# One load for the filter of two blocks, the last block's h turned by transfers, and a new table of places, in a long-convolution and SwiGLU kernel

## The chip, the cores and the metric

The kernel runs on one core of one Trainium2 chip. The core has five engines that run side by side, each through its own queue of instructions in order: TensorE (PE; its weight loads are PEld) multiplies matrices, VectorE (DVE) and ScalarE (ACT) work on elements, GpSimd (POOL) does small things here and issues transfers, SyncE (SP) only issues transfers. An instruction that waits holds up all that stand behind it on its engine, and nothing on the others. Transfers run on 16 DMA engines that all queues share. The metric is the device time of one execution in microseconds (us); lower is better.

## What is computed

The input `A_q` is 2048 rows of 640 channels, in bfloat16. A gated long convolution and a residual give `h`, and a SwiGLU feed-forward on the normalised `h` gives the output:

```
def _A_ref(q, k, v, shift_k, ssm_k, ssm_D):
    ...
        k_shift = k_shift + k_pad[:, t:t + S, :] * shift_k[:, ks - 1 - t][None, None, :]
    kv = k_shift * v
    ...
    y = irfft(rfft(kv padded to 2S) * rfft(ssm_k padded to 2S))[:S]
    y = y + kv * ssm_D[None, None, :]
    return q * y
def _B_ref(x, w_gate, w_up, w_down):
    g = _silu(x @ w_gate)
    u = x @ w_up
    return (g * u) @ w_down
h = x + _A_ref(_layernorm(x), A_k, A_v, A_shift_k, A_ssm_k, A_ssm_D)
h2 = h + _B_ref(_layernorm(h), B_w_gate, B_w_up, B_w_down)
```

(The transforms are written shorter here than in the source.) D is 640, the hidden width F is 1728.

## The kernel before

The 2048 rows are cut into 4 blocks of 512 (`NB`, `BLK`). For each block j the kernel computes a spectrum `G{j}` of the filter `A_ssm_k` and a spectrum `X{j}` of `kv`, both as products with a cosine and sine basis on TensorE (`forward`, line 324) that ScalarE or VectorE copies out of the accumulators (`taken`, line 310: the casts and activations of line 319). `window` joins the spectra of two neighbouring filter blocks to `H{j}`. `mac` (line 524) multiplies: block j needs the sum over i of `X{i}` times `H{j-i}`, so block 0 has one pair and block 3 has four. `inverse` (line 651) goes back to rows with products on TensorE (line 698), then takes the gate, the residual and the statistics of the second normalisation. `turn_h` (line 717) normalises the four row groups of h and lays channels on partitions (`hT`), and `ffn` (line 751) does gate and up (line 769), silu and product (lines 783 to 787), and down (lines 833 and 845). The feed-forward of block j-1 is written beside the convolution of block j, so that TensorE has work while the other engines prepare the next block.

Nothing of this order is left to a compiler. Each step is an entry of `Plan`, and the table `ORDER` (line 47) lists the entries in the order in which they are emitted; every engine runs its own in that order. A negative entry takes the step's other form, on another engine: a copy out of the accumulators goes from ScalarE to VectorE, a load goes from SyncE's to GpSimd's queue, and an addition on VectorE becomes a transfer from GpSimd's queue that adds into its destination:

```
    def added(ns, fn, to, what, reads, write, n=1):
        plan.add("dve", ns, fn, reads, [write], ("add", 2 * P * R * D * n, lambda: nc.gpsimd.dma_start(out=to(), in_=what(), accum_op=ALU.add, ...)))
```

Such an adding transfer (line 243 in the profile) moves 128 x 2560 bfloat16 elements, 655,360 bytes, within SBUF. `mac` is the main user of `added`, through `plus` (line 544; line 545 where it stays on VectorE). For block 3 it makes two strings of additions that each wait for the one ahead: six into the half-size buffer `acc`, and six into the accumulator `A`, three into each of its parts:

```
                    if not i:
                        plus(total, parts[1][0], acc, parts[1][1])
                ...
                for get, at in parts[:1] if final else parts:
                    plus(total, get, acc, at)
                    ...
                        plus(lambda sin=sin: A.part(sin), lambda b=b: flat2(b), A.at(sin), b)
            dve(1402, lambda: v.tensor_sub(A.part(0), A.part(0), A.part(1)), [A.at(1)], [A.at(0)])
            dve(1402, lambda: v.tensor_add(A.part(1), total(), parts[1][0]()), [acc, parts[1][1]], [A.at(1)])
```

The terms that are added are products of `one` (line 542). After the last two lines (581 and 582), `inverse` takes a difference and a sum (662 and 663), two more of half the size (674) and two of the same size (677) before its products can read.

The filter of block j comes by `load_g` (line 289), channels on partitions, 512 columns of 2 bytes, so rows of 1 KB. `g_turned` (line 415) lays time on partitions. For block 0 TensorE turns it (`transposed`, line 411, with a copy out at line 413); for blocks in `GTURN` ScalarE first reorders the whole block (line 419) and SyncE issues four transposing transfers (`turns`, line 404). `HTURN` says the same for h: blocks 1 and 2 are turned by transfers, blocks 0 and 3 by TensorE. Buffers come from an arena of 22 units, and accumulators (`ps`) from four tiles.

Of the kernel before, what the change touches and what calls it, by code (L numbers as in the profile page):

```python
# [16 lines left out]
D = 640  # L17
FF = 1728
P = 128
BLK = 512  # L20
NB = S_TOT // BLK
R = BLK // P
L = 2 * BLK
EPS = 1e-5
KT = D // P
# [14 lines left out]
HTURN = (1, 2)  # L40
# [151 lines left out]
def kernel(ctx: ExitStack, tc: tile.TileContext, A_q, A_k, A_v, A_shift_k, A_ssm_k, A_ssm_D, B_x,  # L192
# [9 lines left out]
             "scr": ("p (a d) -> p a d", {"a": 4}), "hT": ("p (k t) -> p k t", {"k": KT}),  # L202
# [11 lines left out]
    def new(kind):  # L214
        return Buf("U", kind, None, 2 if kind == "S" else 1) if kind in views else Buf(kind, kind)
# [71 lines left out]
    def load_g(j):  # L287
        b = new("ld")
        load(MB, lambda q: q.dma_start(
            out=ap(b).rearrange("p (c t) -> p c t", c=KT),  # L290
            in_=A_ssm_k[0:D, j * BLK:(j + 1) * BLK].rearrange("(c p) t -> p c t", p=P)), [b])
        return b
# [113 lines left out]
    def transposed(pieces, reads, to, write):  # L406
# [5 lines left out]
        pe(290, tr, reads + [ident], [pt])  # L412
        evict(lambda copy: copy(to(), turned(pt)[:, 0:D].rearrange("p (c t) -> p c t", c=KT)), [pt], [write], other=407)

    def g_turned(g, j):
        gT = new("t4")
        if j in GTURN:
            by_r = new("scr")
# [572 lines left out]
```

## Time and profile before

| what | value |
|---|---|
| device time, median of 3 runs (lowest, highest) | 251.36 us (251.21, 253.07) |
| profiled execution, span from first to last instruction | 251.4 us |
| granted TensorE clock, mean | 1.000 |
| busy: PE, DVE, ACT, POOL | 237.3, 197.7, 173.9, 54.0 us |
| instructions: PE, DVE, ACT, POOL | 2113, 249, 300, 54 |
| DMA: GpSimd's queue, SyncE's queue | 11.96 MB, 21.38 MB |
| their packets' time, as a share of 16 engines' span | 25.9%, 32.1% |

The profile is one execution taken by the hardware profiler, so its times add up to its own span of 251.4 us, which here is the median of the runs within 0.1 us. Busy times overlap. A busy TensorE is not one at its peak, since matmuls are pipelined and a slow one counts as busy. A view of waits gives what ended the idle time ahead of an instruction; the chain of waits goes back from the last instruction, at each step to what released it. The view of stretches gives the busy time of each engine in a piece of the span, with the count of its instructions in brackets.

### The profile page before, as it was taken

What the parts mean: (1) busy time and instruction counts of PE and PEld (TensorE: products, weight loads), DVE (VectorE), ACT (ScalarE), POOL (GpSimd) and SP (SyncE); (2) the same over time, 40 slices, a digit from 0 to 9 for tenths busy, and PEclk for the clock granted to TensorE, in tenths of its full rate; (3) what the DMA queues carried; (4) which work ended last, traced back from release to release, by engine and by line L of the source; (5) the groups of instructions that cost most, each with busy time, mean ns of one, the idle gap of its engine ahead of it and who ended that gap; (6) DMA issues with size and microseconds to landing.
All of it is one profiled execution on the core that took longest, in us unless ns stands there. A gap on an engine that the chain in (4) does not pass through costs nothing.

```text
span 251.4 us, 5138 instructions
## 1 busy us (share of the span) xinstructions
PE 237.3 (94%) x2113; PEld 153.0 (61%) x2125; DVE 197.7 (79%) x249; ACT 173.9 (69%) x300; POOL 54.0 (21%) x54
## 2 busy tenths in 40 slices
PE   3869997999999999999999999999999999999994
PEld 3447675788777677444465676454456785465662
DVE  2379999999999999999999989999999542131222
ACT  2449998999999976975988789983542865325100
POOL 0002003231540313220270404263612110000030
PEclk9999999999999999999999999999999999999999
DMA  5995699774998654685345468889592200000052
GB/s 156 376 212 163 127 324 352 231 197 92 165 246 292 202 81 81 105 154 133 79 66 146 86 99 194 148 146 163 98 224 29 26 0 3 0 0 3 0 78 78
DMA packets 37283, 33.66 MB, mean 134 GB/s; under 512 B 22470, under 2 KB 32076, under 8 KB 37260
## 3 DMA queue, kind: packets, MB, share of 16 engines
q1 hardware_dynamic: 31884, 21.38, 32.1%
q0 software_dynamic: 5376, 11.96, 25.9%
q8 instruction: 16, 0.26, 0.4%
q14 instruction: 7, 0.06, 0.1%
HBM read 16.29 MB, written 4.59 MB: 83 GB/s over the span
## 4 chain that ended last, share of the span: by engine, by line
PE 56%; ACT 17%; DMA 10%; DVE 9%; issue 4%; SPq 3%; DVEq 0%; ACTq 0%; POOLq 0%
PE ps L769 24%; PE ps L845 22%; ACT arena L319 7%; DMA arena<-in_A_ssm_k_dram 7%; PE ps L698 5%; DMA arena<-arena 3%; ACT sg L785 2%; PE ps L490 2%; SPq L404 2%; ACT junk L606 1%; PE ps L329 1%; PE ps L833 1%; DVE arena L674 1%; DVE arena L663 1%; DVE arena L662 1%
## 5 line engine op out<-in xcount | busy, mean ns | idle before, releaser
L769 PE MATMUL ps<-arena,wgu 128*128 128x512 bf16 (+1 forms) x668 | 116.7, 328 | 1.4 <-ACT sg L809 0.5
L769 PEld LDWEIGHTS <-wgu 128*128 128x128 bf16 x680 | 66.2, 98 | 45.3 <-issue 1.4
L845 PE MATMUL ps<-wd,tT 128*128 128x320 bf16 x416 | 59.1, 299 | 0.0
L845 PEld LDWEIGHTS <-tT 128*128 128x128 bf16 x416 | 39.8, 98 | 17.2 <-issue 1.8
L542 DVE TENSOR_TENSOR arena<-arena 128x2560 bf16<-128x2560 bf16 x30 | 44.1, 1484 | 0.2
L783 ACT ACTIVATE sg<-ps 128x1024 bf16<-128x1024 f32 (+1 forms) x28 | 26.9, 968 | 20.3 <-PE ps L769 19.7
L329 PE MATMUL ps<-arena,WF 128*128 128x320 bf16 x176 | 29.8, 299 | 1.2 <-ACT arena L319 0.9
L785 ACT CAST sg<-ps 128x1024 bf16<-128x1024 f32 (+1 forms) x23 | 23.0, 998 | 6.9 <-PE ps L769 3.1
L319 ACT CAST arena<-ps 128x320 bf16<-128x320 f32 (+1 forms) x48 | 25.2, 583 | 1.9 <-DVE arena L545 1.1
L610 POOL TENSOR_TENSOR sm<-sm,neghalf 128x4 f32<-128x4 f32 (+1 forms) x10 | 16.6, 1659 | 43.4 <-DVE sm L646 43.1
L787 DVE TENSOR_TENSOR tT<-sg,sg 128x1024 bf16<-128x1024 bf16 (+1 forms) x23 | 15.5, 673 | 11.5 <-ACT sg L785 11.5
L243 POOL DMA_DIRECT2D arena<-arena x11 | 13.3, 1211 | 47.4 <-DVE arena L542 11.2
L329 PEld LDWEIGHTS <-WF 128*128 128x128 bf16 x176 | 17.1, 98 | 10.0 <-issue 2.3
L606 ACT ACTIVATE junk<-arena 128x640 bf16<-128x640 bf16 x28 | 20.8, 744 | 1.3 <-DVE arena L709 1.3
L545 DVE TENSOR_TENSOR arena<-arena 128x2560 bf16<-128x2560 bf16 x14 | 20.7, 1487 | 0.2
L319 ACT ACTIVATE arena<-ps 128x640 bf16<-128x640 f32 (+1 forms) x32 | 20.2, 655 | 0.3
L698 PE MATMUL ps<-arena,WI 128*128 128x320 bf16 x96 | 15.7, 299 | 0.9 <-issue 0.6
L850 ACT ACTIVATE row<-ps,sm 128x640 bf16<-128x640 f32 x12 | 9.5, 791 | 8.2 <-PE ps L845 8.0
L709 DVE SCALAR_TENSOR_TENSOR arena<-arena,sm,ps 128x640 bf16<-128x640 bf16 x16 | 13.6, 876 | 1.8 <-ACT ps L707 1.8
L852 POOL DMA_DIRECT2D out_dram<-row x12 | 11.7, 1153 | 14.1 <-ACT row L850 14.1
L707 ACT ACTIVATE ps<-ps,sm 128x640 f32<-128x640 f32 x16 | 12.1, 770 | 3.7 <-PE ps L698 3.5
L698 PEld LDWEIGHTS <-WI 128*128 128x128 bf16 x96 | 9.0, 97 | 5.6 <-issue 1.3
(91 smaller groups left out, 240.8 us busy)
## 6 DMA issues: line engine op xcount, KB each, us to landing
arena<-arena POOLq DMA_DIRECT2D x11, 640.0 KB, 6.1
arena<-in_A_q_dram SPq DMA_DIRECT2D x4, 640.0 KB, 5.1
out_dram<-row POOLq DMA_DIRECT2D x13, 160.0 KB, 4.2
arena<-in_A_ssm_k_dram SPq DMA_DIRECT2D x3, 640.0 KB, 9.4
arena<-in_A_v_dram SPq DMA_DIRECT2D x3, 640.0 KB, 6.3
wd<-in_B_w_down_dram SPq DMA_DIRECT2D x2, 800.0 KB, 7.3
out_dram<-arena POOLq DMA_DIRECT2D x2, 640.0 KB, 5.8
wgu<-in_B_w_gate_dram SPq DMA_DIRECT2D x1, 800.0 KB, 6.5
```

Source lines behind the costliest of these rows:

```text
L319: (lambda: nc.scalar.activation(dst(), src(), ACT.Copy, scale=2.0)) if twice else (lambda: nc.scalar.copy(dst(), src())),
L329: nc.tensor.matmul(ap(ps)[:, h, 0:NH], w, ap(src)[:, r, h * NH:(h + 1) * NH], start=(first and i == 0), stop=(last and i == len(rs) - 1), ...
L542: dve(1402, lambda: v.tensor_mul(to(), X.part(xs), H.part(hs)), [X.at(xs), H.at(hs)], [at])
L545: added(1402 * n - 69 * (n - 1), lambda: v.tensor_add(to(), to(), b()), to, b, [what], at, n)
L606: act(725, lambda r=r: nc.scalar.activation(waste(), ap(x)[:, r, :], ACT.Square, scale=D ** -0.5, accum_out=sm(s, MSQ, (r,))), [(x, r)], [ ...
L610: nc.gpsimd.tensor_tensor(sm(s, RSTD, rs), sm(s, VAR, rs), ap(neghalf)[:, 0:len(rs)], op=ALU.pow)
L698: nc.tensor.matmul(ap(ps)[:, w, 0:NH], m, src[:, w * NH:(w + 1) * NH], start=(i == 0), stop=(i == len(terms) - 1))
L769: nc.tensor.matmul(split(ap(ps), n)[:, i, :], w(k), ap(hT)[:, k, lo:lo + n], start=(k == 0), stop=(k == KT - 1))
L783: act(905 if wide_ else 490, lambda: nc.scalar.activation(of(sg), of(*gate), ACT.Silu), [(gate[0], gate[1] + i) for i in range(m)] + (psu ...
L785: op = plan.add("act", 905 if wide_ else 490, lambda: nc.scalar.copy(of(co), of(*up)), psu + [sg], [co] + tt, ("dve", 1135 if wide_ else 6 ...
L787: op.rest = dve(602 if wide_ else 336, lambda: nc.vector.tensor_mul(to(), of(sg), of(co)), [sg, co], tt)
L845: nc.tensor.matmul(ap(ps[hf])[:, hf, 0:NH], ap(tT)[:, c * BLK + at:c * BLK + at + P], ap(wd)[:, c, hf * NH:(hf + 1) * NH], start=False, st ...
```

## The change

Three things are changed in the code, and the table `ORDER` is another one throughout, with 918 entries for 923.

- `load_g(0)` loads the filter of blocks 0 and 1 together, 1024 columns, in rows of 2 KB, into a buffer of two arena units. `load_g(1)` falls away, and both `g_turned` calls read halves of that buffer.
- Block 3 joins `HTURN`: the 20 transposes of its h on TensorE and four copies out of the accumulators go, and SyncE issues four transposing transfers in their place.
- The table has new places, and other entries are negative. Of the additions, 25 are adding transfers where 11 were; of those, block 3 has 11 where it had 6 (and its `window` had one more). VectorE keeps 3 of the 14 additions of `plus`. The loads of `x` for block 0, of both halves of `WF` and of one of `WI`, of four of the five pieces of `w_down` and of two of the six of the gate and up weights are issued from GpSimd's queue; SyncE issued all of them. Copies out of the accumulators that ScalarE did, nine of line 319's, are on VectorE.

```
-HTURN = (1, 2)
+HTURN = (1, 2, 3)
...
 ORDER = (
-    0, 1, 2, 3, 16, 18, -20, 5, 4, 8, 17, 186, 9, 20, 22, 7, 10, 11, -22, 24, -26, 23, 26, 75, 76, 13, 15, 12, 6,
...
+    8, 16, 17, 26, 0, 1, 3, 9, 18, 19, 20, 10, 24, 7, 11, 5, -26, 22, 21, -24, 75, 12, 192, 6, 76, 36, 77, 78, 79,
...
+             "pair": ("p (c t) -> p c t", {"c": KT}), "scr": ("p (a d) -> p a d", {"a": 4}), "hT": ("p (k t) -> p k t", {"k": KT}),
...
-        return Buf("U", kind, None, 2 if kind == "S" else 1) if kind in views else Buf(kind, kind)
+        return Buf("U", kind, None, 2 if kind in ("S", "pair") else 1) if kind in views else Buf(kind, kind)
...
     def load_g(j):
-        b = new("ld")
-        load(MB, lambda q: q.dma_start(
-            out=ap(b).rearrange("p (c t) -> p c t", c=KT),
-            in_=A_ssm_k[0:D, j * BLK:(j + 1) * BLK].rearrange("(c p) t -> p c t", p=P)), [b])
-        return b
+        n = 2 if j == 0 else 1
+        b = new("pair" if n > 1 else "ld")
+
+        def at(i=0):
+            t = ap(b) if n > 1 else ap(b).rearrange("p (c t) -> p c t", c=KT)
+            return t[:, :, i * BLK:(i + 1) * BLK]
+        load(n * MB, lambda q: q.dma_start(
+            out=ap(b) if n > 1 else at(),
+            in_=A_ssm_k[0:D, j * BLK:(j + n) * BLK].rearrange("(c p) t -> p c t", p=P)), [b])
+        return [(b, lambda i=i: at(i)) for i in range(n)]
...
-    gT = g_turned(g, 0)
+    gT = g_turned(g[0], 0)
...
-        g = load_g(j)
+        g = g[1:] or load_g(j)
```

Two places of the new order matter below. The first is GpSimd's queue from the load of block 3's `v` to the end of block 3's `mac`. Before, its rows are these (L243 is the adding transfer, L852 the adding store of one row group of the output, L634 to L636 and L610 belong to the normalisation):

```order
L296 DMA arena<-in_A_v_dram 128x2560
L243 DMA arena<-arena 128x2x1280 x3
L634 TENSOR_TENSOR sm_83<-sm_83 128x4
L635 TENSOR_TENSOR sm_83<-sm_83 128x4
L636 TENSOR_SCALAR sm_83<-sm_83 128x4
L610 TENSOR_TENSOR sm_83<-sm_83,neghalf 128x4
L243 DMA arena<-arena 128x2x1280 x2
L852 DMA out_dram<-row_68 128x640
L243 DMA arena<-arena 128x2x1280
```

Six adding transfers stand there. In the changed kernel the same piece of GpSimd's queue (L301 is the load of `v`, L243 the adding transfer, L858 the adding store) reads:

```order
L301 DMA arena<-in_A_v_dram 128x2560
L858 DMA out_dram<-row_68 128x640
L243 DMA arena<-arena 128x2x1280 x3
L858 DMA out_dram<-row_67 128x640
L243 DMA arena<-arena 128x2x1280 x3
L858 DMA out_dram<-row_65 128x640
L243 DMA arena<-arena 128x2x1280 x5
L858 DMA out_dram<-row_64 128x640
```

Eleven stand there: all six of `acc`'s string and five of the six into `A`, with three of the output's stores between them.

The second place is the start of ScalarE's queue. Before (L419 reorders block 1's filter for its turning, L413 and L319 copy out of accumulators, L871 is a dummy silu that pulls in its table):

```order
L871 ACT_TABLE_LOAD
L871 ACTIVATE junk<-bn 128x1
L413 COPY kT<-ps_75 128x5x128
L419 COPY arena<-arena 128x2560
L413 COPY arena<-ps_73 128x640
L319 ACTIVATE arena<-ps_72 128x320
L319 ACTIVATE arena<-ps_73 128x320
```

And in the changed kernel (L418, L425, L324 and L877 are the same steps as L413, L419, L319 and L871):

```order
L418 ACT_TABLE_LOAD
L418 COPY kT<-ps_73 128x5x128
L418 COPY kT<-ps_74 128x5x128
L425 COPY arena<-arena 128x2560
L324 ACTIVATE arena<-ps_74 128x320
L877 ACT_TABLE_LOAD
L877 ACTIVATE junk<-bn 128x1
L324 ACTIVATE arena<-ps_75 128x320
```

The dummy silu and a table load moved from the very start to behind the first copy out of block 0's spectra, and the reordering of block 1's filter, which now reads the shared load, stands ahead of all of these copies.

More of the change, by code (lines that the diff above doesn't have):

```diff
@@ L201 @@
     views = {"x": ("p (r d) -> p r d", {"r": R}), "t4": ("p (r d) -> p r d", {"r": R}), "ld": (None, None), "early": (None, None),
-             "scr": ("p (a d) -> p a d", {"a": 4}), "hT": ("p (k t) -> p k t", {"k": KT}),
+             "pair": ("p (c t) -> p c t", {"c": KT}), "scr": ("p (a d) -> p a d", {"a": 4}), "hT": ("p (k t) -> p k t", {"k": KT}),
              "minus": ("p (a q) -> p a q", {"a": 5}), "S": ("p (h a d) -> p h a d", {"h": 2, "a": 4})}
@@ L413, in transposed, with g_turned @@
         evict(lambda copy: copy(to(), turned(pt)[:, 0:D].rearrange("p (c t) -> p c t", c=KT)), [pt], [write], other=407)
-    def g_turned(g, j):
+    def g_turned(loaded, j):
+        g, g_at = loaded
         gT = new("t4")
@@ L419, in g_turned @@
             act(2414, lambda: nc.scalar.copy(ap(by_r).rearrange("q a b -> q (a b)").rearrange("q (r c p) -> q r c p", r=R, c=KT),
-                                             ap(g).rearrange("q (c p r) -> q r c p", c=KT, r=R)), [g], [by_r])
+                                             g_at().rearrange("q c (p r) -> q r c p", r=R)), [g], [by_r])
             for r in range(R):
@@ L425, in g_turned @@
             for r in range(R):
-                transposed(lambda c, r=r: ap(g).rearrange("q (c p r) -> q c p r", c=KT, r=R)[:, c, :, r], [g],
+                transposed(lambda c, r=r: g_at().rearrange("q c (p r) -> q c p r", r=R)[:, c, :, r], [g],
                            lambda r=r: ap(gT)[:, r, :].rearrange("p (c q) -> p c q", c=KT), (gT, r))
@@ L939 @@
         x = load_x(j)
-        gT = g_turned(g, j)
+        gT = g_turned(g[0], j)
         if not last:
```

82 rows, old and new, of the table ORDER are left out of this document.

## The prediction

> **What bounds the kernel now.** I read the view of stretches first, cut where the work changes (columns: stretch, length, busy PE with its count, PEld, DVE, ACT, POOL, clock, DMA share, GB/s):
>
> ```profile
> 4.40:6.20 1.80, 1.80 (x20) 1.59 (x19) 1.39 (x6) 0.05 (x1) 0.00 (x0) 1.00 0.59 151
> 7.00:14.00 7.00, 4.98 (x147) 2.89 (x146) 3.17 (x7) 2.50 (x1) 0.00 (x0) 1.00 1.04 385
> 15.00:45.20 30.20, 28.22 (x342) 19.64 (x343) 28.87 (x54) 27.96 (x66) 3.92 (x3) 1.00 0.85 230
> 45.20:128.00 82.80, 81.92 (x702) 55.37 (x706) 80.90 (x82) 73.41 (x123) 22.81 (x19) 1.00 0.67 155
> 128.00:194.40 66.40, 65.85 (x531) 38.31 (x534) 64.53 (x65) 46.95 (x78) 22.04 (x22) 1.00 0.68 128
> 194.40:248.00 53.60, 53.39 (x369) 34.47 (x370) 17.06 (x35) 20.90 (x31) 4.64 (x6) 1.00 0.11 20
> ...
> 53.75:56.50 2.75, 2.74 (x28) 2.34 (x27) 2.75 (x2) 2.75 (x4) 0.00 (x0) 1.00 1.10 196
> ```
>
> From 15 to 194 TensorE and VectorE are both full; after 194 only TensorE is, and DMA is nearly idle. The chain of waits (start, us, what) gives the pace of TensorE and the places that matter:
>
> ```profile
> 3.90 11.01 DMA arena<-in_A_ssm_k_dram
> 14.91 0.05 issue
> 14.96 1.03 PE ps L411 x15
> ...
> 82.20 7.17 PE ps L845 x52
> ...
> 170.11 10.14 PE ps L769 x47
> ...
> 185.22 0.38 PE ps L833 x4
> ...
> 194.60 1.09 PE ps L698 x8
> ...
> 200.31 1.36 PE ps L845 x10
> 201.67 0.56 PE ps L411 x10
> ...
> 206.32 0.28 PE ps L411 x5
> ...
> 207.14 0.28 PE ps L411 x5
> ...
> 247.98 0.55 DVE row L864
> ```
>
> The start hangs on a load of the filter, until 14.91. Late in the kernel a 512-wide product takes 10.14/47 = 0.216 us and a 320-wide one 7.17/52 = 0.138. Block 3's inverse starts at 194.60; from there to the end are 251.4 - 194.6 = 56.8 us of unbroken TensorE work and 3.4 us of tail. In the timeline VectorE hands it over only just in time:
>
> ```profile
> 132.97 0.72 PE L698 MATMUL ps<-arena,WI 128*128 128x320 bf16 x4 [0.18 <-DVE arena L674]
> ...
> 190.58 1.49 DVE L663 TENSOR_TENSOR arena<-arena 128x2560 bf16<-128x2560 bf16 x1
> 192.10 1.56 DVE L674 TENSOR_TENSOR arena<-arena 128x1280 bf16<-128x1280 bf16 x2
> ```
>
> So freeing VectorE can only help as far as TensorE has idle time left, and TensorE must still find block 3's sums ready when it gets to them.
>
> **Turning the last h.** Off TensorE go the three pieces of L411 in the chain: 0.56 + 0.28 + 0.28 = 1.12 us, on the path. Added are four transposing transfers from SyncE:
>
> ```profile
> arena<-row SPq DMA_TRANSPOSE x8, 2.7
> ```
>
> They land 2.7 us after issue, four in a row on one queue. Behind SyncE's copies only stores of the end are queued. What hides them is the down projection of block 2: in the new order 8 us of TensorE's products (at the paces above) lie between block 3's last inverse product and the first gate product that reads h, and 11 us until the first that reads the later row groups. Today the stretch from the last inverse product (200.31) to the last transposes (207.14) is 6.8 us; the transfers make it about 6.8 + 2 x 1.3 + 2.7 - 0.6 = 11.5. I take 0, with up to 1 us lost. The result is -1.1 us, between -1.1 and 0.
>
> **Additions that become transfers.** The new order takes 14 further additions off VectorE:
>
> ```profile
> L545 DVE TENSOR_TENSOR arena<-arena x14: 1479/1487/1493, 62.1 to 184.1; 128x2560 bf16<-128x2560 bf16 x14
> ...
> L243 POOL DMA_DIRECT2D arena<-arena x11: 1177/1197/1277, 51.3 to 178.5; - x11
> ...
> DMA to landing us min/median/max: 5.7/6.1/8.1
> ```
>
> VectorE is relieved of 14 x 1.487 = 20.8 us. Against that, one link of a string of additions takes 5.7 to 8.1 us from issue to landing instead of 1.49. And the transfers need the DMA engines: the stretch 53.75 to 56.50 has one of them alone, at 196 GB/s with the DMA engines full, so each holds all 16 for 655,360 bytes / 196 GB/s = 3.35 us; 14 more are 47 us. Spread over the span this fits; in one string it doesn't have to. The place where it decides is block 3.
>
> When does TensorE get there? In the new order 28 forward products and 25 gate and up products that stood ahead of block 2's inverse stand behind it, so that comes at 132.97 - 28 x 0.138 - 25 x 0.216 = 123.7. 52 of L845 and 4 of L833 that stood ahead of block 3's inverse stand behind it: 52 x 0.138 + 0.38 = 7.6 us. Without a new wait it would start at 194.6 - 7.6 = 187.0, and the end would come 56.8 + 7.6 - 1.1 = 63.3 us later, at 250.3.
>
> When are the sums ready? From block 2's inverse to the last product of block 3's filter spectrum the new order has 16 products of L698, 30 of the gate and up and 32 forward ones, 13.1 us: 136.8. A last copy out of the accumulators takes about 1.5 us with its queue:
>
> ```profile
> L319 ACT ACTIVATE arena<-ps 128x640 bf16<-128x640 f32 (+1 forms) x32 | 20.2, 655 | 0.3
> ```
>
> Then VectorE has five operations of 1.49 us (difference, two of `window`, two products) and about 1 us of small ones before the first sum: 136.8 + 1.5 + 7.4 + 1 = 146.7, and with the start's +1 from below 147.7. Six links follow, each after the other: 6 x 6.1 = 36.6, so 184.3 (with 5.7 each 181.9, with 8.1 each 196.3). The five transfers into `A` go between them on the same queue; all eleven need 11 x 3.35 = 36.9 us of the DMA engines, as long as the string itself, so a link will at times find one ahead of it. I add 4.5 us, between 0 and three such packets, 10 us: 188.8. Behind it VectorE does L582, L662, L663 and L674 twice, 3 x 1.49 + 1.56 = 6.0 us: block 3's inverse starts at 194.8, with TensorE there at 188.0 and waiting 6.8 us, all that stands behind it waiting too. **Sum:** 194.8 + 63.3 = 258.1.
>
> One sentence of the Trainium skill would price the links otherwise: "DMA: Bandwidth & Descriptors", section "Anatomy of one DMA", has about 2.0 us and the bytes at 436 GB/s for a transfer from GpSimd, an estimate of 3.5 us for these 655,360 bytes. The rows have 5.7 at the least, so the trace does not agree; by the page the sum would be 250.3.
>
> **The start.** The shared load brings 1311 KB in one piece and nothing of block 0's or 1's filter can start before all of it. Ahead of it SyncE's queue has 1.31 MB (k and v). Alone and at the 385 GB/s of 7.00 to 14.00 these 2.62 MB land at about 9.5. But GpSimd's queue now sends 3 MB in the same stretch (x, WF, WI, pieces of w_down, v): at equal shares it is 2 + 5.2/0.385 = 15.6, with all of them ahead 17. I take 15, nearest to today's 14.91. Behind the landing ScalarE now does this:
>
> ```profile
> 0.79 1.28 ACT L871 ACT_TABLE_LOAD   x1 [0.79 <-PEq L975]
> 2.08 0.20 ACT L871 ACTIVATE junk<-bn 128x1 bf16<-128x1 f32 x1
> ...
> 9.41 2.50 ACT L419 COPY arena<-arena 128x2560 bf16<-128x2560 bf16 x1 [2.57 <-DMA arena<-in_A_ssm_k_dram]
> ...
> 16.30 1.37 ACT L319 ACTIVATE arena<-ps 128x320 bf16<-128x320 f32 x3
> ```
>
> Today the 2.50 us and the table load lie in idle time ahead of 14.9, and copying starts at 16.30; in the change it starts at 15 + 2.5 = 17.5 and loses 1.5 more to the table, 2.7 us in all, with every copy of blocks 0 and 1 queued behind. Copies moved to VectorE give back some 1.7 (three at 0.655). I take +1, between -4.5 (landing at 9.5) and +4. The rows of 2 KB are meant for the stretch 4.40 to 6.20, where loading in 1 KB rows ran at 151 GB/s with the DMA engines 59% busy. The Trainium skill speaks against a gain there: the same page's section "Specifications" gives 512 B as enough for the line rate, and by it the first range would start near 14, not 9.5. The row at 151 GB/s leaves room for a gain, though it may be the queue's filling.
>
> **The weights.** Pieces of w_down go ahead of gate and up weights on GpSimd's queue, and SyncE's first loads of these stand behind transposing transfers of block 1's k and block 2's filter, which wait for other engines. Today the first product of the feed-forward is at 45.23:
>
> ```profile
> 45.23 2.89 PE L769 MATMUL ps<-arena,wgu 128*128 128x256 bf16 x25 [0.16 <-ACT arena L413]
> ```
>
> It waits for a copy, not for weights. 1.4 MB more ahead of them are 1.4/0.230 = 6 us at this stretch's rate. I take 0, since not all weights are needed at once, with up to +4.
>
> **The rivals.**
> 1. *The string delays block 3* (forecast, 0.62): 258.1; 251 with links of 5.7, nothing between them and block 3 beginning 2 us sooner; 263 with three collisions.
> 2. *Only the front is late* (0.08): weights or the shared load cost 3 to 5 us and the string is on time: 253.3 to 255.3. For it: DMA is 0.85 to 1.04 full until 45. Against: TensorE has work of blocks 0 and 1 to go on with.
> 3. *No new wait* (0.15): a link costs little beyond its packets, 6 x 3.35 = 20.1, so the sums are ready by 174 and TensorE sets the end: 250.3, or 251.3 with the start. Against it stands the minimum of 5.7 over eleven transfers. The skill's fit would give this case.
> 4. *The start decides, and it is faster* (0.15): the shared load runs at 385 GB/s and lands before 11, every later step comes 4 us sooner, and the string, begun at 142.7, ends by 177 with links of 5.7; 142.7 + 34.2 + 6.0 = 182.9 is just when TensorE arrives. Then 250.3 - 4 = 246.3. It decides at a landing of about 12 and no collisions in the string; GpSimd's loads in the same stretch speak against it.
>
> **How the numbers follow.** The profile's span is the median of the runs (251.4 and 251.36), so sums carry over. The likeliest case is the first: 258.1, taken as 258; its own range is 251 to 263. The range 249 to 263 leaves out most of case 4 and a little beyond both ends. About 1% (2.5 us) is what a measurement can tell from no change: faster is under 248.9, slower over 253.9. Slower takes 0.59 of case 1 and 0.06 of case 2: 0.65. Within 1% takes 0.03, 0.02, 0.15 and nothing of case 4: 0.20. Faster is case 4: 0.15.
>
> **What would show it.** Right: adding transfers back to back on GpSimd between 148 and 190, some taking over 7 us to land; VectorE idle behind the last of them; TensorE idle for 5 to 10 us ahead of block 3's L704, waiting for VectorE; 63 us from there to the end. Right at the start: the first turning of the filter at 15, the table load among the copies after it. Wrong: block 3's inverse at 187 with no gap ahead of it, or a filter that lands before 12. An idle TensorE between 45 and 125 would say that the delay sits in earlier blocks or the weights.

## The result and the profile after

The changed kernel takes 306.16 us (304.67 to 308.96 over four runs) where the kernel before takes 251.36: a ratio of 1.218, 95% interval 1.211 to 1.225. The forecast was 258.1 with a range of 249 to 263. The direction was right, and the size, 6.7 us forecast against 54.8 measured, was not. Ratios here are taken from the executions within 1.5% of a kernel's shortest one.

The profiled execution has a span of 303.0 us, 51.6 more than before. TensorE is busy for 251.3 us (237.3 before), although it has 20 transposes fewer, and idle for 303.0 - 251.3 = 51.7 us (251.4 - 237.3 = 14.1 before). So 37.6 us are new idle time and 14.0 are longer busy time, at a mean granted clock of 0.927 where it was 1.000. The view of stretches of the changed kernel, cut at its own block boundaries, shows where (columns as in the prediction; the clock is the one granted to TensorE, as a share of the full one):

```profile
15.00:45.00 30.00, 19.70 (x179) 13.44 (x180) 21.35 (x41) 20.28 (x44) 3.06 (x4) 0.81 0.83 221
45.00:80.00 35.00, 30.94 (x327) 22.90 (x326) 25.00 (x35) 26.57 (x46) 13.19 (x9) 0.87 0.93 206
80.00:128.00 48.00, 41.42 (x441) 30.43 (x440) 39.35 (x47) 36.81 (x72) 16.30 (x15) 0.96 0.74 151
128.00:160.00 32.00, 27.18 (x124) 12.74 (x128) 24.68 (x23) 16.48 (x24) 11.30 (x11) 0.89 0.94 173
160.00:200.00 40.00, 38.00 (x376) 23.66 (x378) 33.82 (x39) 27.50 (x53) 12.80 (x11) 1.00 0.70 131
200.00:237.00 37.00, 26.19 (x107) 11.16 (x108) 23.24 (x21) 10.14 (x13) 8.60 (x10) 0.83 0.77 132
237.00:303.00 66.00, 60.74 (x404) 38.71 (x405) 16.37 (x32) 21.92 (x32) 6.15 (x8) 0.99 0.16 31
```

Before, TensorE and VectorE were both full from 15 to 194 at a clock of 1.00. Now TensorE is nearly full in one stretch ahead of 237 (160 to 200) and VectorE in none, and the clock is below 1.00 in all but one. No single stretch holds the loss. The view of TensorE's waits (us in total, times, longest) has these six totals as its longest:

```profile
PE ps L775 <- DMA arena<-row: 9.8, 2, 8.0
PE ps L416 <- DMA arena<-in_A_ssm_k_dram: 8.5, 1, 8.5
PE ps L775 <- DVE tT L792: 5.2, 1, 5.2
PE ps L496 <- DMA kT<-in_A_k_dram: 4.4, 2, 3.5
PE ps L839 <- ACT sg L791: 3.7, 1, 3.7
PE ps L775 <- DMA wgu<-in_B_w_gate_dram: 3.2, 1, 3.2
```

The chain of waits of the changed kernel, at the places of the prediction's steps:

```profile
2.59 17.41 DMA arena<-in_A_ssm_k_dram
...
62.67 4.66 POOL sm L616
67.33 4.73 DMA wgu<-in_B_w_gate_dram
...
123.13 9.22 DMA arena<-row
...
173.68 7.17 issue
180.85 0.04 POOLq L243
180.89 0.54 POOL out_dram L858
181.43 1.56 POOL arena L243
...
190.27 6.08 DMA arena<-arena
...
197.35 10.43 DMA arena<-arena
...
208.31 5.69 DMA arena<-arena
...
214.30 6.70 DMA arena<-arena
...
221.53 7.03 DMA arena<-arena
```

The shared load lands at 20.0. The weights are issued behind statistics on GpSimd's queue and land at 72.1. A transposing transfer for block 1's h takes 9.22 us. Block 3's string of additions starts at 181.4 and ends at 228.6. The 7.17 us ahead of it are no work: in the timeline GpSimd's queue stands behind an adding store that waits for its row.

```profile
180.87 0.87 POOL L858 DMA_DIRECT2D out_dram<-row  x1 [7.19 <-ACT row L856]
```

A mechanism that the prediction did not have is in the timeline of VectorE, behind the string, and in that of TensorE:

```profile
210.74 0.69 DVE L793 TENSOR_TENSOR tT<-sg,sg 128x1024 bf16<-128x1024 bf16 x1
217.46 1.49 DVE L548 TENSOR_TENSOR arena<-arena 128x2560 bf16<-128x2560 bf16 x1 [6.04 <-DMA arena<-arena]
218.87 1.22 DVE L792 TENSOR_TENSOR tT<-sg,ps 128x1024 bf16<-128x1024 bf16 x1
```

```profile
220.14 7.79 PE L775 MATMUL ps<-arena,wgu 128*128 128x512 bf16 x25 [5.23 <-DVE tT L792]
```

L548 is a product of two spectra (L542 of the kernel before) and reads no sum. By the code it writes into a scratch buffer dealt from the arena, and its wait ends when an adding transfer lands, so the buffer it was dealt must be one that this transfer was still reading. L792, a feed-forward product that needs nothing of this, stands behind it on VectorE, and TensorE's next gate products wait for the accumulators that L792 empties. The view of line L243 (the adding transfers) adds it up in us and times: landings are slower than before (5.7/6.1/8.1), and those products waited 18.5 us on them.

```profile
  DVE arena L548: 18.5, 8
...
DMA to landing us min/median/max: 5.7/7.0/10.4
```

### The profile page after: what moved, and what is told of

It reads as the page before. It is cut to its first block, busy times and chain, and to the rows that moved or that the text cites. A ratio compares the mean times of both kernels' runs of the same rounds, so it can differ in the third digit from the quotient of the medians.

```text
span 303.0 us, 5113 instructions
## 1 busy us (share of the span) xinstructions
PE 251.3 (83%) x2094; PEld 157.8 (52%) x2105; DVE 188.8 (62%) x246; ACT 162.3 (54%) x282; POOL 77.6 (26%) x83
## 4 chain that ended last, share of the span: by engine, by line
PE 35%; DMA 33%; issue 9%; DVE 8%; ACT 7%; POOL 4%; SPq 3%; POOLq 0%; DVEq 0%; ACTq 0%
DMA arena<-arena 19%; PE ps L775 17%; PE ps L851 7%; DMA arena<-in_A_ssm_k_dram 6%; DMA arena<-row 5%; PE ps L704 4%; PE ps L334 4%; POOL sm L616 2%; SPq L409 2%; DMA kT<-in_A_k_dram 2%; DMA wgu<-in_B_w_gate_dram 2%; ACT junk L612 1%; ACT ps L713 1%; ACT arena L324 1%; DVE tT L793 1%
## 5 line engine op out<-in xcount | busy, mean ns | idle before, releaser
L775 PE MATMUL ps<-arena,wgu 128*128 128x512 bf16 (+1 forms) x669 | 125.1, 344 | 20.5 <-DMA arena<-row 8.0
L775 PEld LDWEIGHTS <-wgu 128*128 128x128 bf16 x680 | 69.2, 102 | 71.2 <-issue 23.2
L548 DVE TENSOR_TENSOR arena<-arena 128x2560 bf16<-128x2560 bf16 x30 | 44.3, 1488 | 18.7 <-DMA arena<-arena 18.5
L243 POOL DMA_DIRECT2D arena<-arena x25 | 31.4, 1274 | 81.8 <-DMA arena<-arena 30.6
L791 ACT CAST sg<-ps 128x1024 bf16<-128x1024 f32 (+1 forms) x19 | 18.4, 967 | 29.9 <-DVE tT L793 13.0
L324 ACT CAST arena<-ps 128x320 bf16<-128x320 f32 (+1 forms) x45 | 23.3, 577 | 1.0 <-PE ps L334 0.9
L793 DVE TENSOR_TENSOR tT<-sg,sg 128x1024 bf16<-128x1024 bf16 (+1 forms) x19 | 12.5, 660 | 13.7 <-ACT sg L791 13.7
L324 ACT ACTIVATE arena<-ps 128x640 bf16<-128x640 f32 (+1 forms) x26 | 16.1, 644 | 3.9 <-PE ps L334 3.8
L704 PE MATMUL ps<-arena,WI 128*128 128x320 bf16 x96 | 17.1, 323 | 0.0
L858 POOL DMA_DIRECT2D out_dram<-row x12 | 12.9, 1264 | 13.1 <-ACT row L856 13.1
L792 DVE TENSOR_TENSOR tT<-sg,ps 128x1024 bf16<-128x1024 bf16 (+1 forms) x9 | 9.9, 1100 | 9.9 <-ACT sg L789 6.6
L425 ACT COPY arena<-arena 128x2560 bf16<-128x2560 bf16 x3 | 7.6, 2543 | 13.6 <-DMA arena<-in_A_ssm_k_dram 13.6
```

What stands on the lines that cost most here:

```text
L324: (lambda: nc.scalar.activation(dst(), src(), ACT.Copy, scale=2.0)) if twice else (lambda: nc.scalar.copy(dst(), src())),
L548: dve(1402, lambda: v.tensor_mul(to(), X.part(xs), H.part(hs)), [X.at(xs), H.at(hs)], [at])
L704: nc.tensor.matmul(ap(ps)[:, w, 0:NH], m, src[:, w * NH:(w + 1) * NH], start=(i == 0), stop=(i == len(terms) - 1))
L775: nc.tensor.matmul(split(ap(ps), n)[:, i, :], w(k), ap(hT)[:, k, lo:lo + n], start=(k == 0), stop=(k == KT - 1))
L791: op = plan.add("act", 905 if wide_ else 490, lambda: nc.scalar.copy(of(co), of(*up)), psu + [sg], [co] + tt, ("dve", 1135 if wide_ else 6 ...
L793: op.rest = dve(602 if wide_ else 336, lambda: nc.vector.tensor_mul(to(), of(sg), of(co)), [sg, co], tt)
```

## The experiments

"Inverse" in this table of the main kernels is where the timeline has the first product of a block's inverse, "first feed-forward" that of L769 or its later number; all in us of the profiled execution, beside the measured median (the chain has before's last one 0.2 later). Differences below are taken against the kernel before in the same comparison, 251.5 to 252.2 us.

| kernel | median | span | first feed-forward | inverse 1 | inverse 2 | inverse 3 |
|---|---|---|---|---|---|---|
| before | 251.36 | 251.4 | 45.2 | 75.6 | 133.0 | 194.4 |
| changed | 306.16 | 303.0 | 60.0 | 98.5 | 156.9 | 237.0 |
| a_adds_back | 296.84 | 293.4 | 57.7 | 92.4 | 149.8 | 227.4 |
| b_adds_over | 325.14 | 324.3 | 44.5 | 94.0 | 179.3 | 267.3 |
| b_adds3_over | 279.05 | 277.8 | 44.5 | 74.9 | 132.2 | 220.8 |
| p_only | 297.53 | 297.4 | 58.5 | 93.0 | 147.3 | 232.0 |
| a_loads | 307.43 | 304.7 | 52.4 | 97.2 | 158.2 | 238.8 |
| q586 | 280.73 | 279.4 | 44.1 | 74.5 | 131.9 | 213.9 |

**The additions in the changed kernel.** Fifteen entries of the table change sign (a_adds_back), or only block 3's five (a_adds3_back), for instance in this row. The other form of entry n is written as -n - 1, so -691 is entry 690 as a transfer:

```
-    699, 706, 768, 771, 700, 609, 780, 785, 763, -691, -696, 761, 784, -692, 711, 753, 783, 786, -703, 787, 697,
+    699, 706, 768, 771, 700, 609, 780, 785, 763, 690, -696, 761, 784, -692, 711, 753, 783, 786, -703, 787, 697,
```

> The changed kernel with the 15 additions that it alone makes by transfer back on VectorE, at their places in the table; all loads, places and the rest stay. Theory 1, the added transfers cost nearly all of the loss: what is left is the late start (5 us) and the wait for block 0's k (4 us), so 258 to 268 us, and block 3's inverse starts before 205. Theory 2, the new places and the loads cost most of it (copies, stores and statistics queued ahead of others, weights late), the transfers little: 285 to 306 us. Between the two, 268 to 285, both count.

Measured: 296.84 us, 1.181 (1.171 to 1.192). Only 9.3 of 54.8 us come back, which is the second theory.

> The changed kernel with only block 3's five additions back on VectorE. The prediction's view, block 3's string is where the loss is made: the string of 47 us (181.4 to 228.6 in the changed kernel) shrinks to some 10 to 25, TensorE's stops after 193 (14 us) and the low clock behind them (5 us) go, so 280 to 288 us. Rival, the string only fills time that TensorE needs anyway for what it is behind with: 295 us or more.

Measured: 304.97 us, 1.214 (1.207 to 1.220): the rival, and within the spread of the changed kernel's own runs. Block 3's inverse starts at 236.8, where it did with the transfers. So in the changed kernel the forecast's string is not what holds the time.

**The additions in the kernel before.** The same entries get the other sign in the table before, all fifteen (b_adds_over) or block 3's five (b_adds3_over).

> The kernel before with the same 15 additions made into transfers, at the places of its own table; no load and no place is changed. Theory 1, the transfers are what costs: 275 to 300 us, block 3's sums some 25 to 40 us later and TensorE stopped ahead of each block's inverse. Theory 2, places and loads cost: under 262 us.

Measured: 325.14 us, 1.294 (1.287 to 1.301), even more than the theory said.

> The kernel before with only block 3's five further additions as transfers, at its own places. Theory, the forecast's price taken at these places: five links of 6.1 to 8 us in place of 1.49 on a string that was just in time, 23 to 33 us, so 274 to 284 us. Rival, VectorE's relief of 7.4 us and other work between the links take most of it: 252 to 262 us.

Measured: 279.05 us, 1.105 (1.096 to 1.115): the theory. Its views of waits, VectorE's and TensorE's, show the same mechanism as above (L542 is the product, L581 the difference behind the string, L785 and L787 the feed-forward):

```profile
DVE arena L542 <- DMA arena<-arena: 19.4, 4, 8.0
...
DVE arena L581 <- DMA arena<-arena: 9.7, 1, 9.7
```

```profile
PE ps L769 <- ACT sg L785: 10.0, 1, 10.0
PE ps L845 <- DVE tT L787: 5.4, 1, 5.4
```

So at the old places the transfers are dear: 73.6 us for fifteen, 27.1 for five. At the new places the same fifteen cost 9.3. Whether the new places make room for them or other waits hide them can't be told from this; the next runs show what the places cost by themselves.

**The places alone.** p_only is the code of the kernel before (own loads, h by TensorE) with every step in its old form, in the order of the new table; the steps that the new code lacks (the second filter load, the transposes of h) stand where their successors do. The table's first row:

```
-    0, 1, 2, 3, 16, 18, -20, 5, 4, 8, 17, 186, 9, 20, 22, 7, 10, 11, -22, 24, -26, 23, 26, 75, 76, 13, 15, 12, 6,
...
+    8, 16, 17, 26, 0, 1, 3, 9, 18, -20, 20, 10, 24, 7, 11, 5, -26, 22, -22, 23, 75, 12, 186, 193, 6, 76, 36, 77, 78,
...
```

> The code of the kernel before, with its two loads, its h of block 3 turned by TensorE, and every step in its old form (additions, copies, loads on the old engines and queues), only the places of the new table. Theory 1, the forms are the loss (transfers, queues of the loads, the shared load): under 262 us. Theory 2, the places alone make each block's chain wait: 280 to 300 us, with the new forms then giving little of it back.

Measured: 297.53 us, 1.180 (1.170 to 1.190). The order alone costs 45 us, as the second theory had it. The engines issue in that order and the buffers are dealt out in it; nothing else differs. From 2.00 us to block 2's inverse TensorE is busy as long as in the kernel before (121.8 us, 122.8 before), but idle for 23.6 us where it was 8.2. The longest totals in the view of its waits:

```profile
PE ps L768 <- ACT sg L782: 8.1, 1, 8.1
PE ps L328 <- ACT arena L318: 6.4, 8, 2.3
PE ps L328 <- DMA WF<-const_wf: 5.5, 1, 5.5
```

In part these are other stops than the changed kernel's, which has no wait for `WF` and whose 8.5 us for the shared load are not here. So the 45 us can't be taken off the 54.8 to price the rest.

**Which part of the order.** Tables put together from the two: t_fa380 has the new one up to block 1's inverse, the others the old one up to block 1's (q364f, q364) or block 2's inverse (q586f, q586), with the new forms (f) or the old. In effect, for q586f (`OLD` and `NEW` are the two tables in the same numbers):

```
+CUT = OLD[:586]
+ORDER = CUT + tuple(i for i in NEW if max(i, ~i) not in {max(k, ~k) for k in CUT})
```

> The other way round: the first 380 entries of the new table (up to block 1's inverse, with the seven transfers of its additions), then the rest in the order and forms of the table before. Theory, delays add up and nothing is made good later, since TensorE is full there: block 1's inverse at 98 where it was 75.6, and 251.4 + 23 = 274, 270 to 278 us. Rival, the later order has slack to take some of it back: under 266 us.

Measured: 278.22 and 283.28 us in its two runs, at the upper end of the theory's range and above it, so 27 us or more. The profile is of the longer run; in it block 1's inverse starts at 104.0, where the changed kernel has 98.5 and the kernel before 75.6. Those 22.9 us of delay are less than what even the shorter run lost, so nothing is made good.

> The code of the kernel before (own load for each filter, block 3's h turned by TensorE), the first 364 entries of its table (up to block 1's inverse), then the places and forms of the new table. Theory, each stretch adds its own delay: from block 1's inverse to the end the changed kernel took 204.5 us where the kernel before took 175.8, so 251.4 + 28.7 = 280, 275 to 285 us. Rival, the prediction's, only block 3's string of transfers costs in this part: 256 to 264 us.

Measured: 287.31 us, 1.142 (1.135 to 1.149), above the theory's range.

> The same with the old forms (additions, copies and loads on the old engines). Theory, the places alone carry this part's loss: 275 to 285 us. Rival, the transfers carry it: 252 to 262 us.

Measured: 287.37 us, 1.142 (1.135 to 1.149), above its range too. The forms make no difference there.

> The code of the kernel before and the first 586 entries of its table (up to block 2's inverse), then the places and forms of the new table. From block 2's inverse to the end the changed kernel took 146.1 us where the kernel before took 118.4, of which 9.3 us are TensorE's work that the new table moved behind that point. Theory, this part's places and strings cost by themselves: 251.4 + 27.7 - 9.3 = 270, 264 to 276 us. Rival, the prediction's string alone: about 258 us, under 262.

Measured: 281.94 and 287.79 us in its two runs, both above the theory's range.

> The same with the old forms. Theory, places alone: 264 to 278 us. Rival, the transfers are this part's loss: 251 to 257 us.

Measured: 280.73 us, 1.116 (1.108 to 1.123), again a little above the range and close to q586f's shorter run. From block 2's inverse on, the new places alone cost 29 us, with no further transfer. The timelines of VectorE, ScalarE and TensorE in q586 show one of the stops:

```profile
193.17 0.69 DVE L786 TENSOR_TENSOR tT<-sg,sg 128x1024 bf16<-128x1024 bf16 x1
```

```profile
193.95 1.02 ACT L782 ACTIVATE sg<-ps 128x1024 bf16<-128x1024 f32 x1 [9.35 <-DVE tT L786]
```

```profile
195.03 16.11 PE L768 MATMUL ps<-arena,wgu 128*128 128x512 bf16 x64 [8.25 <-ACT sg L782]
```

L786, a feed-forward product, stands on VectorE behind twelve microseconds of `mac` and spectrum steps, from 180.7, without a gap. ScalarE's silu waits for the buffer that L786 frees, and TensorE for the accumulators that the silu frees. It is the mechanism seen above, with VectorE's own order in the transfer's place, and the 8.1 us of p_only's first row is the same wait (it ends at 213.19 there). The parts on either side of block 1's inverse cost 27 and 36 us, together more than the 54.8 of the whole. So they don't add up. A delay in one may be hidden in part by waits in the other, and each seam between two tables may add waits of its own; the runs don't tell these apart. Which entries of the table would have to move was not tried.

**The loads and the front.** a_loads puts all 19 loads whose queue differs back on their old queue, and t_fb228 replaces the first 228 places by the old ones. An edit in a_loads (13 and 14 are the loads of `WF`, 15 that of the skip vector, 27 that of `x`):

```
-    -38, 80, 81, 82, -15, 38, -40, 34, 195, -36, 32, 96, -16, 97, 2, 40, 113, 114, -42, 88, -90, -28, 98, 99, -14,
+    -38, 80, 81, 82, 14, 38, -40, 34, 195, -36, 32, 96, 15, 97, 2, 40, 113, 114, -42, 88, -90, 27, 98, 99, 13,
```

> The changed kernel with every load on the queue where it was before (GpSimd's early ones back behind the shared load on SyncE's), places unchanged. Theory, sharing the DMA engines with GpSimd's early loads is what makes the shared load late: it lands by 10 to 12 in place of 20.0, and 8 to 15 us go: 290 to 298 us. Rival, only the first landing is sooner and SyncE's queue, longer now, holds up what follows: 303 us or more.

Measured: 307.43 us, 1.220 (1.210 to 1.230). It is the rival in its time. In its chain the shared load lands at 11.7, and the first feed-forward product is 7.6 us sooner, but block 1's inverse is only 1.3 us sooner (97.2 for 98.5). `WF`, now behind the shared load on SyncE's queue, comes late, and TensorE waits 5.5 us for it at 15; later a link of block 1's string takes 11.1 us:

```profile
2.60 9.10 DMA arena<-in_A_ssm_k_dram
...
77.80 11.12 DMA arena<-arena
```

> The changed kernel's code with another table: the first 228 entries of the table before (up to the first feed-forward product), then all the rest in the new table's order with its forms. Theory, delays add up: the first feed-forward product is at 45 to 48 where the new table has 60.0, and the end comes 12 to 15 us sooner, 291 to 294 us. Rival, what the front loses is hidden behind later waits anyway: 300 us or more.

Measured: 321.76 us, 1.277 (1.267 to 1.287), outside both. TensorE stops for 14.2 us at 53 in its timeline, where the two tables meet (and the shared load stands at an old place here, as in b_pair); it tells nothing of the front.

The reverse, in the kernel before: its loads on the new queues (b_loads_over), and the shared load alone (b_pair).

> The kernel before with its own places, only the loads moved between SyncE's and GpSimd's queue as the new table has them (19 loads). Theory, a queue that issues in order makes a load on GpSimd wait behind additions and statistics and the other way round: 255 to 270 us, weights or filters late. Rival, queues are interchangeable here: 250 to 253 us.

Measured: 266.00 us, 1.055 (1.047 to 1.063). The view of waits has one new long stop, for gate weights that come late, 9.4 of the 13.9 us lost:

```profile
PE ps L769 <- DMA wgu<-in_B_w_gate_dram: 9.4, 1, 9.4
```

> The kernel before with the shared load of both filters alone, issued where block 1's was, block 0's own load gone. Theory, the shared load is no cost where it is early on its queue: it lands by 11 to 13 us where block 0's own landed at 14.9, so 248 to 251 us. Rival, two units of the buffer held longer, or a load that comes in one piece, delay the start: 253 us or more.

Measured: 264.47 us, 1.053 (1.044 to 1.061): the rival. TensorE's first turning of the filter starts at 13.78, sooner than before's 14.96, but it then stops for 4.2 us at 26.5. The buffers are dealt out anew with the pair. A load on SyncE's queue, issued at 24.92, had waited 9.6 us until forward products (L333) had read its buffer, with block 1's turning transfers behind it. The 4.2 us are a third of the 12.9 lost; the rest was not followed.

**Turning h by transfers.** b_h3 turns all of block 3's h so, at the old places; b_h3_half and b_h3_late two of the four row groups. This is the edit of b_h3_late (b_h3_half has `at > 1`):

```
-            if j in HTURN:
+            if j in HTURN or j == NB - 1 and at < 2:
```

> The kernel before with block 3's h turned by the four transfers, each at the place in the table where TensorE's transposes stood. The prediction takes 1.1 us off TensorE if the transfers are hidden: 250.3 us. Rival: at these places the gate and up products follow closely and wait for the landings, 2.6 to 3.6 us each in the changed kernel: 253 to 256 us.

Measured: 254.91 us, 1.013 (1.010 to 1.017). The timeline of TensorE has the wait, and the view of stretches the clock behind it:

```profile
206.19 5.65 PE L768 MATMUL ps<-arena,wgu 128*128 128x256 bf16 x35 [2.86 <-DMA arena<-row]
```

```profile
206.00:208.00 2.00, 1.81 (x11) 1.38 (x12) 0.00 (x0) 0.22 (x1) 0.00 (x0) 0.63 0.42 82
208.00:210.00 2.00, 2.00 (x11) 1.45 (x10) 0.00 (x0) 0.00 (x0) 0.00 (x0) 0.51 0.42 82
210.00:212.00 2.00, 2.00 (x21) 1.79 (x19) 0.00 (x0) 0.13 (x1) 0.00 (x0) 1.00 0.00 0
```

The 35 products would take 35 x 2.89/25 = 4.05 us at before's pace, so the low clock costs 1.6: -1.12 + 2.86 + 1.6 = 3.3, the measured difference.

> The kernel before with only the last two of block 3's four row groups turned by transfers, the first two still by TensorE. The whole turning by transfers cost 3.3 us, since the first gate product waits for the first two groups. Theory, what is needed first stays on TensorE and the later two are hidden by the products of the first two: 0.28 + 0.28 us off TensorE and no wait, 250.8 us. Rival, the later two still land too late, or the copy they replace was hidden anyway: 251.3 us or more.

Measured: 255.27 us, 1.010 (1.005 to 1.016). The stop is still there, 2.85 us. `at > 1` was the wrong pair: these two groups are the ones needed first.

> The kernel before with two of block 3's four row groups turned by transfers, this time the two that are needed last; the first two by TensorE. Theory, the wait of 2.9 us and the half clock behind it come from the first two groups, and the later two are hidden: 0.56 us off TensorE and no wait, 250.8 us. Rival, the later two are waited for too: 251.5 us or more.

Measured: 252.17 us, 1.000 (0.996 to 1.003). The wait at the first products is gone, one of 1.11 us remains at a later product, and nothing is gained. No version that ran beats the kernel before.

**The clock.** a_hold fills four long waits of the changed kernel with dummy products.

```
+HOLD = {36: 30, 225: 10, 312: 24, 574: 30}
...
+    def hold(dst, a=4):
+        for _ in range(HOLD.get(plan.now, 0)):
+            nc.tensor.matmul(dst.rearrange("p (a b) -> p a b", a=a), ap(ident), ap(ident).unsqueeze(1).to_broadcast([P, a, P]), start=True, stop=True)
```

> The changed kernel with dummy products on TensorE ahead of four products that wait long there (30 ahead of the first turning of the filter, 10 ahead of block 1's convolution, 24 narrow ones ahead of the eighth pair of feed-forward weights, 30 ahead of block 1's feed-forward); each writes where the next product writes afterwards, so nothing else changes. Theory, the half clock follows from TensorE standing still for some 3 us: the granted clock stays 1.0 behind these four waits, where it was 0.81 from 15 to 45 and 0.87 from 45 to 80, and 3 to 9 us go, 297 to 303 us. Rival 1, the clock falls for another reason (transfers at the same time): it stays low and the time is the same or longer, 306 us or more. Rival 2, the clock is full again but the strings of transfers decide the time: clock 1.0 there, and 304 to 306 us.

Measured: 305.15 us, 1.210 (1.202 to 1.217). Its view of stretches has the clock back where the dummies are:

```profile
15.00:45.00 30.00, 25.23 (x212) 15.13 (x210) 21.09 (x41) 20.21 (x44) 3.06 (x4) 0.96 0.82 219
45.00:80.00 35.00, 33.52 (x378) 26.12 (x378) 27.65 (x39) 29.91 (x52) 13.60 (x10) 0.98 0.95 210
```

0.96 and 0.98 in place of 0.81 and 0.87, and the time is the same within the runs' spread: the second rival. With the stops filled the clock is back while the DMA engines are as busy as before (0.82 and 0.95, before 0.83 and 0.93), so the low clock follows TensorE's stops and not the transfers. The time that this saves is taken up by later waits.

## Why the prediction was wrong

**The step that failed is "When does TensorE get there?".** The prediction put block 2's inverse at "123.7" and TensorE's arrival at block 3's inverse at 187.0, by taking the products that moved behind these points off the old times. That holds if everything ahead runs without new waits. It ran to 156.9 and 237.0. In p_only, where all work and all forms are the old ones, the same points are at 147.3 and 232.0. The order itself made TensorE wait, and a sum of work can't show that: by the forecast's count TensorE had 9.3 us less work ahead of block 2's inverse, and in p_only it came 14.3 us later, with 15.4 us more of idle time.

**The string.** Its price was nearly right where it was looked at: a link takes 5.7 to 10.4 us (forecast 5.7 to 8.1), the six with what lies between them 228.56 - 181.43 = 47.1 (forecast 36.6 + 4.5 = 41.1), and alone at the old places the five further transfers cost 27.1. Its start was 33.7 us later than forecast, since block 2's inverse was 33.2 late (1 of them put in for the start); from there to the string's start 24.5 us lie, where 23.0 were forecast, 7.2 of GpSimd's waiting behind a store among them. "VectorE is relieved of 20.8 us" was of no use: products waited 18.5 us for buffers that transfers still read. The prediction counted a transfer's latency in its own string, and not the buffer it holds nor the steps behind the waiting product. Even so, taking block 3's five out gave back 1.2 us, less than the spread of the runs, and block 3's inverse began where it had: other waits stood close behind. So the kernel is slower, as forecast, but not through the string that the forecast gave as the reason; in that sense the right direction is luck.

**The start and the weights.** "+1, between -4.5 and +4" and "0 ... with up to +4" were too small. The landing was 20.0, against 15 taken and 17 as the worst; GpSimd's queue sends block 2's filter (0.66 MB) too, and the sum left it out (1.7 us at the prediction's 385 GB/s, an estimate). TensorE waited 8.5 us there, 4.4 for block 1's k and 3.2 for weights behind GpSimd's statistics. The first feed-forward product came 14.8 us late. The second rival ("only the front is late") had the place right and gave it 3 to 5 us.

**The h turn.** "-1.1, between -1.1 and 0": with the new cover one wait of 1.8 us is left, at the products of the last columns in TensorE's timeline (257.79), so the term is about +0.7. Without that cover it is +3.3.

**The end.** 63.3 us from block 3's inverse to the end were forecast, and 66.0 were measured; with the 1.8 for the wait above it is 65.1, so this term stands within 1 us.

**What no term had is the clock.** The 14.0 us of longer busy time are more than twice the whole forecast loss. They are part of the span as it ran, but a full clock alone would not give them back: a_hold restored it in two stretches, and the time stayed the same. The view of stretches around the wait for weights shows how it goes:

```profile
66.00:70.00 4.00, 2.91 (x26) 2.26 (x24) 3.27 (x3) 4.00 (x7) 3.54 (x3) 1.00 0.64 183
70.00:72.00 2.00, 0.00 (x0) 0.00 (x0) 2.00 (x3) 2.00 (x5) 0.00 (x0) 0.78 1.06 327
72.00:76.00 4.00, 3.90 (x19) 2.71 (x20) 1.36 (x2) 0.71 (x2) 1.21 (x1) 0.50 0.98 182
76.00:78.00 2.00, 2.00 (x12) 1.39 (x11) 2.00 (x2) 0.00 (x0) 1.06 (x1) 0.52 1.11 200
78.00:82.00 4.00, 4.00 (x43) 3.50 (x41) 1.70 (x3) 3.31 (x5) 1.32 (x2) 1.00 0.94 163
```

After 3.2 us of standing still the clock is 0.50 for some six microseconds of work. The Trainium skill has this: "TensorE: Matmul & The Clock Gate", section "Part 1: The HAM clock gate (the "warmup" mystery)", gives half the clock after an idle window of about 3.4 us, and full clock again after about as long of work. The trace agrees with the half and with the kind of delay. It differs on the length, since stops of 2.85 and 2.86 us (b_h3_half, b_h3) were enough, while one of 2.98 in the kernel before (at 12 to 15) left the clock at 1.00. The way back differs too: some six microseconds here, and less than four in b_h3 (206.19 to 210.00). The same section puts the ramp at under 1% of a typical kernel span; here the stops recur, and TensorE's busy time is 14.0 us longer in a span of 303.0.

The signs that the prediction named came out mixed. The slow landings and VectorE's wait behind the string are there; "TensorE idle for 5 to 10 us ahead of block 3's L704" is there too, in pieces (5.2 us at 215, and 3.7 + 1.8 from 228 on). But "an idle TensorE between 45 and 125 would say that the delay sits in earlier blocks or the weights" is what the stretches show, and the 33.2 us by which block 2's inverse was late are the larger part of the miss.

## What to carry to other kernels

When an order is new throughout, a sum of work gives the earliest time at which an engine can arrive, not the time at which it will: with two engines full, walk each queue through the new order and ask of each instruction what it waits for, its buffer included, and who stands behind it. An addition turned into a transfer can cost more than its latency: it holds the buffers that it reads, and the products that need them hold up all that stands behind them on their engine. A stop of TensorE of about three microseconds can also halve the clock for the next four to six (stops of 2.86 and 3.2 us did here, one of 2.98 did not), so count stops, not only their sum; and where waits stand close behind each other, undoing one cause shows little of what it costs.

## What the runs showed of the hardware

Transposing transfers of h land 2.6 to 3.6 us after issue at the end of the changed kernel, where little else moves. Beside adding transfers, at 119 to 132 us of the changed kernel, three of them took 5.9 to 9.2, and TensorE stopped for 8.0 us on them. An adding transfer took up to 12.4 us to land (b_adds_over, one of several issued within 13 us), twice the median of 6.1 before.
